# A's softmax chain at other steps of the block plan: three matches in the block in front, maxima and sums in four pieces, the exponential beside a product

## The chip, the cores and the metric

The kernel runs on one core of one Trainium2 chip. The metric is the device time of one execution in microseconds; of several runs the median is taken. Besides these runs there is one execution taken by the hardware profiler, from which all rows of the profile come. Its engines: PE multiplies matrices (PEld is its loading of weights), DVE is the vector engine, ACT the scalar engine, POOL is GpSimd, SP issues most of the DMA transfers. Each engine works through its own queue in order and waits there for semaphores of the others.

## The reference

Two attentions over inputs of 2048 x 576, with 32 heads of 18, side by side in the output:

```python
# A: each position attends to 8 positions, 2 apart, up to itself
qkv = (x @ wqkv)                       # q, k, v: heads x positions x 18
idx = pos[:, None] - arange(8) * 2     # masked where negative
logits = einsum("bhsd,bhswd->bhsw", q, k[idx]) * scale
o = einsum("bhsw,bhswd->bhsd", softmax(logits), v[idx]);  a = o @ wo
# B: full attention
p = softmax(einsum("bhqd,bhkd->bhqk", q, k) * scale)
o = einsum("bhqk,bhkd->bhqd", p, v);  b = o @ wo
out = concatenate([a, b], -1)
```

A and B have inputs and weights of their own.

## The kernel before

**Three stages.** First come the projections (x times wqkv for A and B), with part of B's maxima between the products. Then the main loop makes B's attention in 512 steps, and beside it, on engines' spare time, A's attention. At the end stand B's last output products.

**B's loop.** The 512 steps are 8 groups of four heads, times 4 blocks of 512 queries, times 16 tiles of 128 keys. A step (the `while step < ALL` loop at the end) makes four score products on PE (`score`, L263) and on ACT an exponential of each (L268); on PE the weighing with v of the step before (`weigh`, L731, all four heads into one PSUM tile `po`); and maxima for a later block: products of q and k on PE (`take`, L160), reduced on DVE (`reduce`, L168), worth three reductions of 128 x 512 a step. Scores, maxima and A's output products share seven PSUM banks in rings, so PE can only go on when ACT or DVE has given a bank back. When the 16 key tiles of a block are through (at steps 16, 32, 48 and so on), `finish` copies `po` out on ACT (L740), and plans the rest at fixed distances: the denominators go through DRAM (`den` loaded 1 step later, reciprocal on DVE 8 later, `drec` stored 9 later, `rec` loaded 13 later), and POOL multiplies and splits 18, 19 and 20 steps later (L767 to L769).

**The plan.** `plan(start, pieces)` and `later(n, f)` put functions on an agenda by step; `due()` runs those of a step at its end. What a function issues is thereby placed in the queues of its engines, behind all that earlier steps placed there. No engine waits for a step as such. POOL, with little of B's, may run ahead of the steps or behind them. SP too runs ahead until a transfer must wait, and what is queued behind that waits with it.

**A's blocks.** `local(j)` plans one of eight blocks of 256 positions, started at step 10 + 54 j. Its steps, counted from there, before the change:

- `fetch`: SP loads q (tile `aq`, one buffer) in four transfers from step -18 on, k (tile `akv`, two buffers, shared with v) from -10 on, and v from 16 on (for block 0: q from -9, k from -5).
- `match(c)`, c from 0 to 8: POOL multiplies q with the window of k (L868) and adds to the sum (L872), both 128 x 1024, at steps 5 to 25; the last makes the logits `lg` (L875, 128 x 512). The sum stays in the first of two `pr` buffers.
- `most`: DVE folds the eight window places into their maximum `am` in three pieces of 256, 128 and 64 elements a partition (L886) at steps 31, 32, 33.
- `lower`: POOL subtracts it (L892), step 33. `exponents`: ACT, one instruction of 128 x 512 (L895), step 35.
- `total`: DVE folds to the sum `as` the same way (L886), steps 36, 37, 38; `inverses`: two reciprocals on DVE (L902), 38 and 39. `share`: POOL multiplies (L905), 39.
- `weighted(c)`: POOL multiplies with v's window (L911) and adds three times (L912 to L914), steps 39 to 59; `upper` and `rest` split the result (L918, L923) at 60 and 61; `put` stores it at 64 and 66.
- `get`, `finished`: per block, four products with `wo` (two halves of columns for each 128 positions) are made at the steps that the table `MADE` names; `get` loads their input 8 steps ahead. `sums_of_a` puts a product into the next step's work, ahead of the fourth score: `beside` (L1036) makes its matrix products with two further maxima among them, ACT copies one sum (L954) and DVE adds the other (L955).

So a piece of A on DVE stands between two of B's reductions in DVE's queue, and one on ACT between two of B's exponentials.

Of the kernel before, what the change touches and what calls it, by code (L numbers as in the profile page):

```python
# [19 lines left out]
DH = 18  # L20
W = 8
# [21 lines left out]
GAP = 54  # L43

A_FROM = 10

MADE = ((88, 96, 112, 128), (144, 160, 176, 192), (201, 208, 224, 240), (250, 256, 272, 288),
        (304, 320, 336, 352), (361, 368, 384, 400), (412, 416, 432, 448), (466, 468, 475, 480))


def ap(t, *dims):

    return bass.AP(tensor=t.tensor, offset=t.offset, ap=[list(t.ap[0])] + [list(d) for d in dims])


def rows(t, *dims):

    return bass.AP(tensor=t.tensor, offset=t.offset, ap=[list(d) for d in dims])
# [3 lines left out]
def two_attentions(ctx: ExitStack, tc, xa, wa, woa, xb, wb, wob, out):  # L62
# [5 lines left out]
    nc = tc.nc  # L68
# [301 lines left out]
    with (tc.tile_pool(name="x", bufs=1, side="right") as xp,  # L370
# [103 lines left out]
        if True:  # L474
# [195 lines left out]
            for k in range(2, 14):  # L670
                n = 46 if k == 2 else 36 + 4 * k
# [7 lines left out]
            def leave_a(c, b, n, ps):  # L679
                o = xp.tile([128, 512], F32, name="ohi", bufs=4)  # L680
                nc.scalar.activation(o[:n], ps, AF.Copy)  # L681
                load(da[128 * c : 128 * c + n, HALO + 512 * b : HALO + 512 * b + 512], o[:n])
# [23 lines left out]
            for c, b in order:  # L706
                n = min(128, 3 * D - 128 * c)
                work_list.append(((b % 2, ws[c][0], xas[b][0], slice(0, n), every),
                                  lambda ps, n=n: ps[:n], lambda ps, c=c, b=b, n=n: leave_a(c, b, n, ps)))
# [109 lines left out]
    wo = {}  # L819

    producing = set()

    def load_wo(k, src, *pieces):

        raw = work.tile([128, D], F32, name="y", bufs=4)
        n = 0
        if len(pieces) == 4:
            nc.gpsimd.memset(raw, 0.0)
            n = 128
        for at, c0, m in pieces:  # L830
            load(raw[at : at + m], src[c0 : c0 + m])
            n = max(n, at + m)
        if k == "a":
            hi = work.tile([128, D], F32R, name="wohi", bufs=5)
            lo = work.tile([128, D], F32R, name="wolo", bufs=5)
        else:

            c = len(wo.get(k, []))
            hi, lo = (ap(t[:, 0, 0, :] if len(t.shape) == 4 else t[:, 0, :], (1, NB * 1024))[:, D * c : D * c + D]
                      for t in sets[(NG - 3) % 3])  # L840
        wo.setdefault(k, []).append((hi, lo))
        later(3, lambda: split_on(nc.gpsimd, hi[:n], lo[:n], raw[:n]))


    def local(j):

        st = {}
# [11 lines left out]
        def window(t, c):  # L859

            return ap(t[:, 2 * c, HALO:], (HALO + SUB, 2), (-DIL, W), (1, SUB))

        def wide():
            return work.tile([128, 2, W, SUB], F32, name="pr", bufs=2)

        def match(c):
            pr = wide()
            nc.gpsimd.tensor_mul(pr, ap(st["q"][:, 2 * c], (SUB, 2), (0, W), (1, SUB)), window(st["k"], c))  # L868
            if c == 0:
                st["pr"] = pr  # L870
            else:
                nc.gpsimd.tensor_add(st["pr"], st["pr"], pr)  # L872
            if c == DH // 2 - 1:
                lg = st["lg"] = work.tile([128, W, SUB], F32, name="lg", bufs=1)
                nc.gpsimd.tensor_add(lg, st["pr"][:, 0], st["pr"][:, 1])  # L875
                if j == 0:
                    for w in range(1, W):
                        nc.gpsimd.memset(lg[:32, w, : DIL * w], MASKED)

        def over_window(op, name, n):  # L880

            if n == 0:
                st[name] = work.tile([128, W // 2, SUB], F32, name=name, bufs=1)
            t, half = st[name], W >> n + 1
            src = t if n else st["lg"]
            nc.vector.tensor_tensor(t[:, :half], src[:, :half], src[:, half : 2 * half], op=op)  # L886

        def most(n):
            over_window(ALU.max, "am", n)
# [17 lines left out]
        def weighted(c):  # L907
            if c == 0:
                st["o"] = work.tile([128, DH, SUB], F32, name="ao", bufs=1)
            at = wide()  # L910
            nc.gpsimd.tensor_mul(at, ap(st["lg"], (0, 2), (SUB, W), (1, SUB)), window(st["v"], c))  # L911
            nc.gpsimd.tensor_add(at[:, :, :4], at[:, :, :4], at[:, :, 4:])  # L912
            nc.gpsimd.tensor_add(at[:, :, :2], at[:, :, :2], at[:, :, 2:4])  # L913
            nc.gpsimd.tensor_add(st["o"][:, 2 * c : 2 * c + 2], at[:, :, 0], at[:, :, 1])  # L914
# [10 lines left out]
        def put(i):  # L925
            load(rows(dao[j, i, 0, 0], (DH * SUB, 128), (1, DH * SUB)),
                 ap(st["parts"][i].bitcast(F32), (1, DH * SUB)))

        def get(n):
            st["x"] = []  # L930
            st["n"] = n
            last = work.tile([128, 128], F32R, name="ahl", bufs=1)
            for i in range(2):
                t = work.tile([128, 4, 128], F32R, name=f"at{i}", bufs=1)
                for s in range(2):
                    load(t.bitcast(F32)[:, :, SUB * s : SUB * s + SUB],
                         dao[j, i, 2 * n + s, :512].rearrange("(c p) n -> p c n", p=128))
                load(last.bitcast(F32)[64 * i : 64 * i + 64].rearrange("p (s n) -> p s n", s=2),
                     rows(dao[j, i, 2 * n, 512], (SUB, 64), (D * SUB, 2), (1, SUB)))
                st["x"].append([t[:, c] for c in range(4)])  # L940
            st["x"].append(last)
# [4 lines left out]
        def sums_of_a(h):  # L946
            his, los = zip(*wo["a"])
            w = his[:4], los[:4], his[4], los[4]
            cols = slice(288 * h, 288 * h + 288)
            if h == 0:  # L950
                st["y"] = ys["a", j, st["n"]] = work.tile([128, D], F32, name="y", bufs=4)
            one, two = beside("scores", *(halves(r, 0, w, st["x"], cols, slice(0, 128), True) for r in range(2)))
            y = st["y"][:, cols]
            nc.scalar.activation(y, two, AF.Copy)  # L954
            behind_scores.append(lambda: nc.vector.tensor_add(y, one, y))  # L955

        pieces = [(33, lower), (35, exponents), (39, share), (60, upper), (61, rest), (64, lambda: put(0)), (66, lambda: put(1))]

        pieces[:0] = [(at, lambda f=f, n=n: f(n)) for f, ats in ((most, (31, 32, 33)), (total, (36, 37, 38)),
                                                                (inverses, (38, 39))) for n, at in enumerate(ats)]  # L960
        for c in range(DH // 2):
            pieces.append((5 + 5 * c // 2, lambda c=c: match(c)))
            pieces.append((39 + 5 * c // 2, lambda c=c: weighted(c)))

        for nm, at, apart in (("q", -18, 2), ("k", -10, 2)) if j else (("q", -9, 1), ("k", -5, 1)):
            pieces += [(at + apart * i, lambda nm=nm, i=i: fetch(nm, i)) for i in range(4)]
        pieces += [(16 + 2 * i, lambda i=i: fetch("v", i)) for i in range(4)]
        made = [p - A_FROM - GAP * j for p in MADE[j]]
        for n, ends in enumerate((made[:2], made[2:])):
            pieces.append((max(ends[0] - 8, made[1] + 1 if n else 0), lambda n=n: get(n)))  # L970
            for h in range(2):
                pieces.append((ends[h], lambda h=h: finished(h)))
                producing.add(A_FROM + GAP * j + ends[h] + 1)
            pieces.append((ends[1] + 6, lambda n=n: load(out[p0 + 128 * n : p0 + 128 * n + 128, :D], ys["a", j, n])))
# [47 lines left out]
    def beside(kind, *both):  # L1022

        sums_ = [bank(k)[:, :288] for k in (kind, None)]
        turns = [[(sums_[r], *ab, i == 0, i == len(t) - 1) for i, ab in enumerate(t)] for r, t in enumerate(both)]
        pair = kind and sum(given) + 2 <= NG * NB * PIECES * 2
        if pair:

            for r in range(2):
                turns[r].insert(6 + 4 * r, None)  # L1030
        for i in range(max(map(len, turns))):
            for r in range(2):
                if i < len(turns[r]):
                    if turns[r][i]:
                        ps, a, b, start, stop = turns[r][i]
                        nc.tensor.matmul(ps, a, b, start=start, stop=stop)  # L1036
                    else:
                        maximum(r)()
        if pair:

            rings["else"].append(rings["else"].pop(0))
        return sums_
# [90 lines left out]
    rest = NG * NB * PIECES * 2 - early  # L1133

    total = early + rest
# [4 lines left out]
    while step < ALL:  # L1140
        n, kt = divmod(step, NT)
# [63 lines left out]
```

## Time and profile before

| | us |
|---|---|
| median of 3 runs | 1619.34 (1617.29 to 1619.95) |
| the profiled execution's own time | 1616.82 |
| its span | 1615.0 |
| PE, ACT, DVE, POOL busy | 1599.0, 1212.4, 1393.9, 961.1 |
| first exponential of the main loop's step 1 | 418.9 |
| first exponential of the last step | 1600.0 |

A row of the page's groups reads: line, engine, operation, tiles (written <- read), shapes and count, then busy us and mean ns of one, then the idle time of the engine just before them and what ended it. Instructions of an engine overlap a little, so busy time over count is less than the mean. In a view by stretches a row is: the stretch in us, its length, busy us and count of each engine that was asked for, the granted clock of PE (1.00 is full), the share of DMA and GB/s. A timeline row is: start, us, engine, line, operation, and in brackets the idle time before it with its releaser.

### The profile page before, as it was taken

Reading aid. Unit: us, or ns where it says so; the run is one execution under the profiler, and the core shown is the slowest. Engines: PE = TensorE matmul, PEld = TensorE weight load, DVE = VectorE, ACT = ScalarE, POOL = GpSimd, SP = SyncE. Lnnn points to the kernel's source line nnn. Section 1 sums busy time; section 2 is a strip of 40 time slices with the busy share of each in tenths; the row PEclk is TensorE's granted clock in tenths of the full one; section 3 lists DMA queues with packets and bytes.
Section 4 is the critical chain, followed back from the end, with each engine's and each line's share of the span. In section 5 each row is a group of like instructions: output and inputs, shape, how many; then the busy total and the mean of one; then the engine's idle time right before and its main releaser. Section 6 shows DMA issues by size and latency. Waiting matters only on the chain.

```text
span 1615.0 us, 35230 instructions
## 1 busy us (share of the span) xinstructions
PE 1599.0 (99%) x13394; PEld 959.5 (59%) x13394; DVE 1393.9 (86%) x2366; ACT 1212.4 (75%) x2419; POOL 961.1 (60%) x792
## 2 busy tenths in 40 slices
PE   9999999999999999999999999999999999999998
PEld 7999888999544444444444444444444444445676
DVE  5199999999899998999999999999999999999532
ACT  6424442121799998999999999999999999998444
POOL 2405742210265995996995995995996997920000
PEclk9999999999999999999999999999999999999999
DMA  8937954432222262254235235332532241034201
GB/s 250 239 121 196 275 164 133 134 104 79 60 56 64 73 147 54 62 118 113 62 85 133 72 98 115 98 91 60 125 106 58 59 135 47 22 124 139 89 38 60
DMA packets 186058, 172.11 MB, mean 107 GB/s; under 512 B 119152, under 2 KB 132976, under 8 KB 184160
## 3 DMA queue, kind: packets, MB, share of 16 engines
q1 hardware_dynamic: 181024, 158.31, 35.3%
q0 software_dynamic: 4032, 10.63, 3.1%
q8 instruction: 105, 1.72, 0.5%
q10 hardware_dynamic: 832, 0.92, 0.2%
q14 instruction: 65, 0.53, 0.1%
HBM read 96.94 MB, written 71.90 MB: 105 GB/s over the span
## 4 chain that ended last, share of the span: by engine, by line
PE 82%; POOL 7%; DVE 5%; DMA 3%; ACT 2%; issue 1%; SPq 0%; POOLq 0%; DVEq 0%; ACTq 0%
PE po L731 24%; PE bank L160 15%; PE bank L353 15%; PE bank L263 15%; PE bank L1036 8%; PE bank L290 5%; DVE mx L168 4%; ACT e L268 2%; POOL pr L868 1%; POOL pr L872 1%; POOL pr L911 1%; DMA akv<-da 1%; DMA dqk<-olo 1%; POOL pr L912 1%; POOL pr L913 0%
## 5 line engine op out<-in xcount | busy, mean ns | idle before, releaser
L168 DVE TENSOR_REDUCE mx<-bank 128x2 f32<-128x512 f32 x2048 | 1286.0, 684 | 114.5 <-PE bank L160 86.2
L268 ACT ACTIVATE e<-bank 128x512 f32<-128x512 f32 x2048 | 1050.2, 607 | 90.3 <-PE bank L263 83.2
L160 PE MATMUL bank<-ks,qs 54*128 54x256 f32 (+1 forms) x2536 | 791.8, 377 | 7.4 <-DVE mx L168 5.9
L160 PEld LDWEIGHTS bank<-ks,qs 54*128 54x128 f32 x2536 | 411.3, 184 | 464.6 <-DVE mx L168 423.4
L263 PE MATMUL bank<-qs,ks 56*128 56x512 f32 x2048 | 567.3, 426 | 0.1
L731 PE MATMUL po<-e,v 128*19 128x512 f32 x4096 | 537.9, 599 | 0.0
L263 PEld LDWEIGHTS bank<-qs,ks 56*128 56x128 f32 x2048 | 299.3, 185 | 14.7 <-issue 7.5
L868 POOL TENSOR_TENSOR pr<-aq,akv 128x1024 f32<-128x1024 f32 x72 | 158.5, 2202 | 15.4 <-DMA akv<-da 12.8
L911 POOL TENSOR_TENSOR pr<-lg,akv 128x1024 f32<-128x1024 f32 x72 | 158.5, 2201 | 0.6
L872 POOL TENSOR_TENSOR pr<-pr 128x1024 f32<-128x1024 f32 x64 | 152.6, 2384 | 5.0
L731 PEld LDWEIGHTS po<-e,v 128*19 128x19 f32 x4096 | 70.5, 97 | 129.4 <-issue 127.0
L681 ACT ACTIVATE ohi<-bank 128x512 f32<-128x512 f32 (+1 forms) x56 | 30.4, 595 | 152.5 <-issue 100.7
L353 PE MATMUL bank<-xhi,ahi 64*128 64x512 f32 (+1 forms) x448 | 113.5, 387 | 0.0
L353 PE MATMUL bank<-xhi,alo 64*128 64x512 f32 (+1 forms) x448 | 112.3, 387 | 0.0
L353 PE MATMUL bank<-xlo,ahi 64*128 64x512 f32 (+1 forms) x448 | 111.9, 388 | 0.1
L912 POOL TENSOR_TENSOR pr<-pr 128x512 f32<-128x512 f32 x72 | 92.5, 1285 | 5.6
L401 POOL TENSOR_TENSOR alo<-raw,ahi 128x512 fp32r<-128x512 f32 (+1 forms) x14 | 17.6, 1258 | 120.7 <-ACT ahi L400 88.8
L493 POOL TENSOR_TENSOR olo<-olo,ohi 128x512 fp32r<-128x512 f32 x36 | 46.2, 1294 | 66.1 <-ACT ohi L492 57.5
L767 POOL TENSOR_TENSOR o<-o,rec 128x512 f32<-128x512 f32 x29 | 37.6, 1297 | 58.7 <-ACT e L268 34.2
L103 POOL CAST mh<-mt 128x32 fp32r<-128x32 f32 x32 | 6.9, 217 | 102.3 <-DVE mt L183 99.5
L353 PEld LDWEIGHTS bank<-xhi,ahi 64*128 64x128 f32 (+1 forms) x448 | 65.0, 181 | 2.9
L353 PEld LDWEIGHTS bank<-xhi,alo 64*128 64x128 f32 (+1 forms) x448 | 63.9, 182 | 2.9
(197 smaller groups left out, 1827.6 us busy)
## 6 DMA issues: line engine op xcount, KB each, us to landing
do<-n SPq DMA_DIRECT2D x28, 512.0 KB
da<-ohi SPq DMA_DIRECT2D x52, 256.0 KB
akv<-da SPq DMA_DIRECT2D x64, 175.5 KB
out<-y SPq DMA_DIRECT2D x32, 288.0 KB
qs<-dqk SPq DMA_DIRECT2D x30, 288.0 KB
ks<-dqk SPq DMA_DIRECT2D x30, 288.0 KB
at<-dao SPq DMA_DIRECT2D x64, 128.0 KB
rec<-drec SPq DMA_DIRECT2D x29, 256.0 KB
```

Source lines behind the costliest of these rows:

```text
L160: return nc.tensor.matmul(ps if part is None else ps[:, 256 * r : 256 * r + 256], qs[at, b, p, 128 * t : 128 * t + 128], ks[at, p, 512 * k ...
L168: nc.vector.tensor_reduce(at, ps.rearrange("q (s n) -> q s n", s=2), axis=AX.X, op=ALU.max)
L263: nc.tensor.matmul(ps, ks[at, p, 128 * kt : 128 * kt + 128], qs[at, b, p], start=True, stop=True)
L268: nc.scalar.activation(e, ps, AF.Exp, scale=SCALE)
L290: nc.tensor.matmul(ps, a, b, start=c == i == 0, stop=c == 4 and i == 1)
L353: nc.tensor.matmul(ps, a, b, start=start, stop=stop)
L731: nc.tensor.matmul(po[32 * i : 32 * i + 19], vs[g][:, kt, 19 * i : 19 * i + 19], es[i], start=kt == 0, stop=kt == NT - 1)
L868: nc.gpsimd.tensor_mul(pr, ap(st["q"][:, 2 * c], (SUB, 2), (0, W), (1, SUB)), window(st["k"], c))
L872: nc.gpsimd.tensor_add(st["pr"], st["pr"], pr)
L911: nc.gpsimd.tensor_mul(at, ap(st["lg"], (0, 2), (SUB, W), (1, SUB)), window(st["v"], c))
L912: nc.gpsimd.tensor_add(at[:, :, :4], at[:, :, :4], at[:, :, 4:])
L1036: nc.tensor.matmul(ps, a, b, start=start, stop=stop)
```

## The change

In block j + 1, matches 0, 1 and 2 move from steps 5, 7 and 10 to -18, -17 and -15, that is to steps 36, 37 and 39 of block j (between `lower` and `share` there); matches 3 to 8 then stand at 11 to 23. Block 0 keeps its matches. The fetches of q and k move to -26 and -25 and on, one of each in turn. The maxima are folded in four pieces at steps 31 to 34 and the sums in four at 38 to 41: 128, 128, 128 and 64 elements in place of 256, 128 and 64. `lower` goes to 34, the exponential to 36, inverses to 42 and 43, share to 43, `weighted` to 43 to 63, `upper` and `rest` to 64 and 65, `put` to 68 and 70; in block 0 all these stand 4 steps earlier. Where `MADE` has a product at the exponential's step, the exponential is issued inside that product, in front of ACT's copy. `MADE` gets other steps for the first products of blocks 0, 3, 5 and 7, and `get` stands 6 steps ahead. Lines behind the new names shift by 3 to 13: `lower` is L897 in the changed kernel, `most` and `total` L890, `match` L871 and L875, `share` L910.

```diff
@@ -44,8 +44,8 @@
 
 A_FROM = 10
 
-MADE = ((88, 96, 112, 128), (144, 160, 176, 192), (201, 208, 224, 240), (250, 256, 272, 288),
-        (304, 320, 336, 352), (361, 368, 384, 400), (412, 416, 432, 448), (466, 468, 475, 480))
+MADE = ((96, 100, 112, 128), (144, 160, 176, 192), (201, 208, 224, 240), (256, 262, 272, 288),
+        (304, 320, 336, 352), (368, 370, 384, 400), (416, 424, 432, 448), (466, 468, 475, 480))
 
 
 def ap(t, *dims):
@@ -819,6 +819,9 @@
     wo = {}
 
     producing = set()
+    MADE_IN = {p for ends in MADE for p in ends}
+
+    beside_product = []
 
     def load_wo(k, src, *pieces):
 
@@ -881,9 +884,11 @@
 
             if n == 0:
                 st[name] = work.tile([128, W // 2, SUB], F32, name=name, bufs=1)
-            t, half = st[name], W >> n + 1
-            src = t if n else st["lg"]
-            nc.vector.tensor_tensor(t[:, :half], src[:, :half], src[:, half : 2 * half], op=op)
+
+            at, size, apart = ((0, 2, 4), (2, 2, 4), (0, 2, 2), (0, 1, 1))[n]
+            t, src = st[name], st[name] if n > 1 else st["lg"]
+            nc.vector.tensor_tensor(t[:, at : at + size], src[:, at : at + size],
+                                    src[:, at + apart : at + apart + size], op=op)
 
         def most(n):
             over_window(ALU.max, "am", n)
@@ -951,23 +956,31 @@
                 st["y"] = ys["a", j, st["n"]] = work.tile([128, D], F32, name="y", bufs=4)
             one, two = beside("scores", *(halves(r, 0, w, st["x"], cols, slice(0, 128), True) for r in range(2)))
             y = st["y"][:, cols]
+            while beside_product:
+                beside_product.pop()()
             nc.scalar.activation(y, two, AF.Copy)
             behind_scores.append(lambda: nc.vector.tensor_add(y, one, y))
 
-        pieces = [(33, lower), (35, exponents), (39, share), (60, upper), (61, rest), (64, lambda: put(0)), (66, lambda: put(1))]
-
-        pieces[:0] = [(at, lambda f=f, n=n: f(n)) for f, ats in ((most, (31, 32, 33)), (total, (36, 37, 38)),
-                                                                (inverses, (38, 39))) for n, at in enumerate(ats)]
-        for c in range(DH // 2):
-            pieces.append((5 + 5 * c // 2, lambda c=c: match(c)))
-            pieces.append((39 + 5 * c // 2, lambda c=c: weighted(c)))
-
-        for nm, at, apart in (("q", -18, 2), ("k", -10, 2)) if j else (("q", -9, 1), ("k", -5, 1)):
+
+        soon = 0 if j else 4
+        in_product = A_FROM + GAP * j + 36 - soon in MADE_IN
+        pieces = [(34, lower), (36, (lambda: beside_product.append(exponents)) if in_product else exponents),
+                  (43, share), (64, upper), (65, rest), (68, lambda: put(0)), (70, lambda: put(1))]
+
+        pieces[:0] = [(at, lambda f=f, n=n: f(n)) for f, ats in ((most, (31, 32, 33, 34)), (total, (38, 39, 40, 41)),
+                                                                (inverses, (42, 43))) for n, at in enumerate(ats)]
+        pieces += [(43 + 5 * c // 2, lambda c=c: weighted(c)) for c in range(DH // 2)]
+        pieces = [(at - soon, f) for at, f in pieces]
+
+        pieces += [(5 + 5 * c // 2 if not j else (-18, -17, -15)[c] if c < 3 else 11 + 5 * (c - 3) // 2, lambda c=c: match(c))
+                   for c in range(DH // 2)]
+
+        for nm, at, apart in (("q", -26, 2), ("k", -25, 2)) if j else (("q", -9, 1), ("k", -5, 1)):
             pieces += [(at + apart * i, lambda nm=nm, i=i: fetch(nm, i)) for i in range(4)]
         pieces += [(16 + 2 * i, lambda i=i: fetch("v", i)) for i in range(4)]
         made = [p - A_FROM - GAP * j for p in MADE[j]]
         for n, ends in enumerate((made[:2], made[2:])):
-            pieces.append((max(ends[0] - 8, made[1] + 1 if n else 0), lambda n=n: get(n)))
+            pieces.append((max(ends[0] - 6, made[1] + 1 if n else 0), lambda n=n: get(n)))
             for h in range(2):
                 pieces.append((ends[h], lambda h=h: finished(h)))
                 producing.add(A_FROM + GAP * j + ends[h] + 1)
```

## Prediction

> **What bounds the kernel now.** I read the head of the page first, then its costliest groups, and then cut the main loop into its steps by the exponentials of B (four `L268` to a step).
>
> ```profile
> span 1615.0 us, 35230 instructions
> ...
> PE 1599.0 (99%) x13394; PEld 959.5 (59%) x13394; DVE 1393.9 (86%) x2366; ACT 1212.4 (75%) x2419; POOL 961.1 (60%) x792
> ...
> L168 DVE TENSOR_REDUCE mx<-bank 128x2 f32<-128x512 f32 x2048 | 1286.0, 684 | 114.5 <-PE bank L160 86.2
> L268 ACT ACTIVATE e<-bank 128x512 f32<-128x512 f32 x2048 | 1050.2, 607 | 90.3 <-PE bank L263 83.2
> ...
> L868 POOL TENSOR_TENSOR pr<-aq,akv 128x1024 f32<-128x1024 f32 x72 | 158.5, 2202 | 15.4 <-DMA akv<-da 12.8
> ...
> L872 POOL TENSOR_TENSOR pr<-pr 128x1024 f32<-128x1024 f32 x64 | 152.6, 2384 | 5.0
> ```
>
> PE's 99% is not the answer: PE, DVE and ACT hand PSUM banks round in a ring, and each stands a little for the next. What a step costs, the busy time of the exponentials alone shows (stretch: us, busy and count, granted clock, DMA):
>
> ```profile
> 668.55:690.93 22.38, 22.38 (x45) 1.00 0.10 37
> 617.16:633.24 16.08, 8.46 (x17) 0.79 0.21 56
> 658.40:668.56 10.16, 8.30 (x17) 1.00 0.18 39
> 862.08:870.27 8.19, 8.11 (x16) 1.00 0.67 184
> 1343.01:1352.16 9.15, 8.23 (x17) 1.00 0.04 8
> 742.49:751.08 8.59, 8.13 (x17) 1.00 0.16 54
> 1100.90:1109.64 8.74, 8.17 (x17) 1.00 0.17 63
> ```
>
> The first row is eleven quiet steps: 22.38 / 11 = 2.035 us each. The others are four steps each, 8.14 when quiet; (the extra exponential in a count is one that the edge cuts). The reductions in the same eleven steps, by the same view cut to `L168`:
>
> ```profile
> 668.55:690.93 22.38, 20.77 (x34) 1.00 0.10 37
> ```
>
> They are 0.61 us each (20.77 / 34), three to a step and one cut by an edge: DVE is busy 1.83 to 1.89 of 2.035 us, so a step has only some 0.15 to 0.2 us of DVE to spare. Blocks of A put their maxima (`am`), sums (`as`) and inverses into that queue, in order with the reductions. The row 862.08 holds all three `am` of one block and costs 8.19 - 8.14 = 0.05: the ring absorbs about 0.9 us of DVE over such a stretch. What goes beyond is paid.
>
> **The dear place** is the second row: 16.08 us for steps 95 to 98, where the like four steps 111 to 114 (a block's start and a product in both) take 10.16. The timeline there, and two stretches of the plain windows:
>
> ```profile
> 621.31 1.26 POOL L875 TENSOR_TENSOR lg<-pr 128x512 f32<-128x512 f32 x1
> ...
> 622.61 0.43 DVE L886 TENSOR_TENSOR am<-lg 128x256 f32<-128x256 f32 x1 [3.38 <-POOL lg L875]
> ...
> 623.68 0.58 PE L160 MATMUL bank<-ks,qs 54*128 54x256 f32 x1 [2.85 <-DVE mx L168]
> ```
>
> ```profile
> 619.00:623.30 4.30, 1.83 (x16) 0.58 (x14) 0.92 (x3) 2.83 (x6) 3.49 (x2) 1.00 0.08 21
> 623.30:630.10 6.80, 6.42 (x41) 5.04 (x45) 4.95 (x9) 2.69 (x5) 0.00 (x0) 0.50 0.21 53
> ```
>
> POOL finishes the logits of A's block 1 too late, DVE stands 3.38 us before `am` with its reductions queued behind, PE stands 2.85, and then the granted clock is 0.50 for 6.8 us. So POOL, busy 60%, is what A's chain runs into.
>
> **What the change removes.** (1) The stall. POOL works without a pause from the share of block 0 to those logits:
>
> ```profile
> 522.06 1.28 POOL L905 TENSOR_TENSOR lg<-lg,as 128x512 f32<-128x512 f32 x1 [7.07 <-ACT e L268]
> ```
>
> The inverses of block 0 stay at steps 48 and 49, so its share stays there; but matches 0 and 1 of block 1 now stand ahead of it, in POOL's 7.07 us pause and the one ahead of `lower`. That is 2.20 + 2.20 + 2.38 = 6.8 us less behind it: the logits end at 622.6 - 6.8 = 615.8. `am` was asked for at 622.61 - 3.38 = 619.2; the product taken out of step 89 brings that to about 617.1 (its 2.07 follows below). POOL is 1.3 us early, and the stall goes: 10.16 - 16.08 = **-5.9**. Next late is what bounds any step, the ring.
>
> (2) The exponentials of a block (`L895`, one of 0.65 us on ACT). Stretches of `L268`, then of `L895`:
>
> ```profile
> 633.24:641.79 8.55, 8.12 (x17) 1.00 0.40 87
> 907.55:913.69 6.14, 4.32 (x9) 1.00 0.02 4
> 1226.98:1233.13 6.15, 4.31 (x9) 1.00 0.23 48
> ```
>
> ```profile
> 1226.98:1233.13 6.15, 0.63 (x1) 1.00 0.23 48
> ```
>
> Without a product (633.24, four steps) they cost 8.55 - 8.14 = 0.41. Beside one (1226.98, two steps of block 6, where it happened already) nothing: 6.15 against 6.14 for the same pair without them; and a product costs 6.14 - 4.07 = 2.07, the block's copy inside it. By step 36 of a block (32 in block 0) and the new table they fall beside a product in blocks 1, 3, 4, 6 and 7: four new ones, **-1.6**. The cover is ACT's idle time while PE makes the product; gone, it is 0.41 again.
>
> (3) `am` against POOL. Of two-input DVE operations that meet a running POOL operation the timeline shows:
>
> ```profile
> 1344.58 1.42 POOL L104 TENSOR_TENSOR ks<-y,qs 126x576 fp32r<-126x576 f32 x1
> ...
> 1344.97 1.31 DVE L886 TENSOR_TENSOR am<-lg 128x256 f32<-128x256 f32 x1
> ...
> 1345.96 1.46 POOL L767 TENSOR_TENSOR o<-o,rec 128x512 f32<-128x512 f32 x1
> ```
>
> `am` takes 1.31 and ends 0.28 after POOL's operation does, where the median of its eight is 0.42 (quoted below): it waits POOL out. Three blocks pay for such a meeting: 9.15, 8.59 and 8.74 above against 8.19, together 1.9. Which POOL operations lie there depends on when B's reciprocals land; POOL being earlier avoids some, not all. I take half, **-1.0**, between 0 and 1.9.
>
> **What it adds.** The `am` and `as` now are four pieces, not three:
>
> ```profile
> L886 DVE TENSOR_TENSOR am<-lg x8: 412/416/1306, 504.3 to 1345.0; 128x256 f32<-128x256 f32 x8
> ```
>
> ```profile
> L886 DVE TENSOR_TENSOR as<-as 128x128 f32<-128x128 f32 x8 | 2.2, 279 | 0.0
> ```
>
> The 0.42 becomes two of 0.28: +0.14 twice in eight blocks, 2.2 us of DVE, over one step more each with 0.15 to spare. I count 0; uncovered, 2.2. The products number as many at a block's start as before (96, 256, 368, 416 stay, the single ones move): 0. Fetches of q and k go 8 and 15 steps earlier in SP's queue, past `den` and reciprocal transfers; the buffer of q is free when match 8 has run, some 3 steps ahead of `lower`; one landing in the chain of waits is
>
> ```profile
> 477.81 5.32 DMA akv<-da
> ```
>
> 5.3 us, so eight issues and a landing end about when `lower` does: 0, with 1 to 3 us of POOL's time if late, which its pauses hold.
>
> **The new meeting.** POOL's pauses were what kept the sums clear of it:
>
> ```profile
> POOL lg L905 <- DVE as L902: 53.3, 6, 11.7
> POOL lg L892 <- DVE am L886: 38.8, 6, 10.5
> ```
>
> Between `lower` and the share POOL was idle 7 to 12 us while DVE made the sums and inverses. Now it goes from `lower` straight into matches 0 to 2 of the next block: 3 x 2.20 + 2 x 2.38 = 11.4 us, in some blocks with B's 3.2 us among them. In block 2 of before
>
> ```profile
> 749.64 1.27 POOL L892 TENSOR_TENSOR lg<-lg,am 128x512 f32<-128x512 f32 x1
> ...
> 755.09 0.42 DVE L886 TENSOR_TENSOR as<-lg 128x256 f32<-128x256 f32 x1
> ```
>
> the first sum comes 4.2 us after `lower` ends, three steps of the plan; now it is four, so 6.2, or with the exponentials in a product 6.2 + 2.07 - 0.41 = 7.9. Both lie inside the 11.4. No row has a two-input DVE operation under a match; the nearest (above) is one under a 1.42 us operation. Bounds: nothing, if it slips between two, and all of 2.38. The first wait I take at its mean, half of 2.3 = 1.15, since 0.3 us of shift turns 0.1 into 2.2. Then DVE's piece and POOL's next operation start together: three reductions later (1.83) the next piece meets the rest of 2.20 or 2.38, about 0.4. Three pieces are caught in blocks 1, 2, 3, 5 and 6 (1.95 each), two in blocks 0 and 4 (1.55), none in 7, which has no next block: 5 x 1.95 + 2 x 1.55 = **+12.9**. Spare DVE time is already used by the pieces themselves, so I let it cost in full, as the row 1343.01 does (0.9 longer for 0.89 more in `am`). Ends: 7 x 0.6 = 4 and 7 x 2.9 = 20.
>
> [...]
>
> **Sum:** -5.9 - 1.6 - 1.0 + 12.9 = +4.4. The profiled execution took 1616.82 us (span 1615.0 and 1.8 around it) and would become 1621.2; the runs' median is 1619.34, 2.5 above it. As the forecast is of a median: 1619.34 + 4.4 = **1623.7 us**.
>
> **Rivals.**
> - *The ring absorbs the waits* (faster). If the 0.4 us waits vanish in the banks' slack, and half a microsecond of the first too, seven blocks pay 0.65 each: 4.5 - 8.5 = -4.0, **1615.3**. For it: the row 862.08, where 0.9 us of DVE costs 0.05. Against: 1343.01. It decides where a block's waits cost below 0.75 us (7 x 0.75 = 8.5 - 3.2). 18%.
> - *They cost about what the rest saves*: 1.2 us a block, 7 x 1.2 - 8.5 = 0, **1619.3**. 27%.
> - *POOL is late again at block 1.* The margin is 1.3 us; match 2 still stands behind the share, and a late landing of k there uses it up. Then -5.9 fails: **1629.6**. 8%.
> - *A wait stops the clock.* After 2.85 us of idle PE it was halved; after the 0.9 us near 1347 it was not (1.00 in 1343.01). A wait of 2.4 lies between. Two such cost 2 x (5.9 - 2.85) = 6: **1629.8**. 5%. [...]
> - The forecast: 42%.
>
> Telling 0.2% (3.2 us) from no change is about what a measurement of this kernel can do. Faster by more 18%, within 27%, slower 55%. Range: from the first rival, 1615, to past the two last, 1630; the far ends of the new waits (4 and 20) would give 1615 and 1631.
>
> **What would show it.** Steps 95 to 98 near 10.2 us and no stretch at clock 0.50: step 1 right. `L897`'s row followed by matches with no pause, and `as` pieces of over 1 us where 0.28 is normal, one to three in each of blocks 0 to 6: the new meeting. If `as` stays at 0.28, the matches do not run there and the first rival or better holds. If `as` is long but four-step stretches stay at 8.2, the ring absorbed it. Wrong altogether would be a long wait of POOL for `akv`, or SP queued behind the early fetches with B's reciprocal late.

## The result, and the profile after

| | before | after |
|---|---|---|
| median of five runs each, on one chip, us | 1617.29 (1615.92 to 1619.95) | **1635.91** (1633.88 to 1640.55) |
| ratio | | **1.0119**, 95% interval 1.0097 to 1.0140 |
| profiled execution, us; its span | 1616.82; 1615.0 | 1633.88; 1632.1 |

The changed kernel is 18.6 us slower. The forecast said slower, but by 4.4, and the time lies above its range.

The head of the page after, two of its groups, and below them four rows of the waits of POOL (what it waited for, us in total, times, longest):

```profile
span 1632.1 us, 35226 instructions
...
PE 1601.4 (98%) x13394; PEld 964.1 (59%) x13394; DVE 1402.9 (86%) x2382; ACT 1212.2 (74%) x2419; POOL 962.4 (59%) x792
...
L871 POOL TENSOR_TENSOR pr<-aq,akv 128x1024 f32<-128x1024 f32 x72 | 158.4, 2203 | 64.4 <-DMA akv<-da 58.8
```

```profile
POOL pr L871 <- DMA akv<-da: 58.8, 6, 22.4
...
POOL lg L897 <- DVE am L890: 42.2, 7, 9.5
...
POOL lg L910 <- DVE as L907: 20.9, 5, 7.2
POOL lg L910 <- DVE mt L183: 17.4, 1, 17.4
```

Busy times are those of before to within a per cent; the time is in waits. The waits of `share` (L905 before, L910 after) fell, as the prediction had it: 53.3 + 7.1 us before, 20.9 + 17.4 after, where the 17.4 is block 7's, which has no next block. Matches now fill that pause. But the matches themselves wait 58.8 us for k where they waited 12.8, once for 22.4.

**Where it comes.** Comparing the first exponential of each step in the two traces, after is 2.2 us ahead at step 112, 2.9 ahead at step 256, 10.9 behind at 272, 16.4 behind at 288, and 17.4 behind at the end. So two short stretches decide. The exponentials of B (`L268`) there, with steps 95 to 98 first, then 256 to 259, and 272 and 273 (columns as in the prediction):

```profile
617.40:627.66 10.26, 8.31 (x17) 1.00 0.83 133
976.41:999.02 22.61, 8.39 (x17) 0.77 0.16 51
1025.82:1037.51 11.69, 4.31 (x9) 0.85 0.75 169
```

The first took 16.08 in before: the stall that the change was predicted to remove is gone. The other two are new: 22.61 and 11.69, where such steps with a product take 10.2 and 6.14.

**The chain behind the first of them** begins 120 us earlier, with the transfers of block 4's q and k. SP's own timeline:

```profile
856.86 0.62 SPq L858 DMA_DIRECT2D aq<-da  x1
...
858.11 0.60 SPq L858 DMA_DIRECT2D akv<-da  x1
860.27 2.67 SPq L142 DMA_DIRECT2D ks<-dqk  x1
...
869.31 0.56 SPq L858 DMA_DIRECT2D akv<-da  x1
...
876.88 2.38 SPq L766 DMA_DIRECT2D rec<-drec  x1
...
880.17 2.69 SPq L858 DMA_DIRECT2D akv<-da  x1
882.96 3.43 SPq L763 DMA_DIRECT2D den<-o  x1
```

These eight fetches are planned at steps 200 to 207. At steps 193 to 204 the plan also has the twelve loads of B's group 5 (`stack_loads`, `L142` and `L143`, 288 KB each; the expectations below say sixteen), in the same queue. The last five of them stand between the fetches. So the eight issues reach from 856.86 to 882.86. Single issues last 1.9 to 2.7 us in place of 0.6 (two of the loads, `rec` and the last fetch), and in front of loads SP itself waits, by its view of waits from 856.8 to 882.9, for the landing of earlier loads:

```profile
SPq L142 <- DMA ks<-dqk: 4.2, 2, 2.4
SPq L142 <- DMA qs<-dqk: 3.4, 2, 1.9
```

The POOL timeline shows what waits for the last fetch:

```profile
868.63 1.28 POOL L897 TENSOR_TENSOR lg<-lg,am 128x512 f32<-128x512 f32 x1 [8.96 <-DVE am L890]
892.31 2.17 POOL L871 TENSOR_TENSOR pr<-aq,akv 128x1024 f32<-128x1024 f32 x1 [22.40 <-DMA akv<-da]
...
907.33 1.27 POOL L910 TENSOR_TENSOR lg<-lg,as 128x512 f32<-128x512 f32 x1
```

`lower` of block 3, then 22.40 us of nothing, then match 0 of block 4; and behind the three matches the `share` of block 3, which needs nothing of k. Its last input, an inverse on DVE, was there at 888.91 (the reciprocal at 888.57, 0.34 long); it ran at 907.33. POOL works in order, so block 3 is 18.4 us late from here on, `weighted` and all. At step 256 B's own copy on ACT, `o` (`L740`), meets a POOL that has not yet freed its buffer:

```profile
982.81 0.60 ACT L740 ACTIVATE o<-po 128x512 f32<-128x512 f32 x1 [4.31 <-POOL n L769]
```

```profile
976.00:983.00 7.00, 2.88 (x23) 1.29 (x23) 2.98 (x5) 2.69 (x6) 6.86 (x6) 0.89 0.00 0
983.00:990.00 7.00, 7.00 (x52) 5.09 (x56) 3.13 (x5) 3.35 (x8) 6.76 (x4) 0.62 0.30 112
```

(Plain windows: PE, PEld, DVE, ACT, POOL, clock.) PE works 2.88 of 7 us while POOL is busy 6.86: POOL is the bound here, as ACT's exponentials stand behind `o` in its queue. In the second row PE is busy all through, at a clock of 0.62. Directly behind come the logits of block 4, late in their turn. The waits view from 970 to 1040 has that wait and those of PE:

```profile
DVE am L890 <- POOL lg L878: 4.7, 1, 4.7
...
PE bank L160 <- ACTq L243: 4.1, 1, 4.1
PE bank L160 <- DVE mx L168: 4.0, 1, 4.0
PE bank L1049 <- DMA at<-dao: 3.5, 2, 2.9
```

At 272 the product waits 2.9 us for its input (`at<-dao`, `L1049`), and PE's clock drops once more, to 0.50 from 1033 to 1036.

### The profile page after: what moved, and what is told of

Same layout as the page of the kernel before. It is cut to its first block, busy times and chain, and to the rows that moved or that the text cites. A ratio compares the mean times of both kernels' runs of the same rounds, so it can differ in the third digit from the quotient of the medians.

```text
span 1632.1 us, 35226 instructions
## 1 busy us (share of the span) xinstructions
PE 1601.4 (98%) x13394; PEld 964.1 (59%) x13394; DVE 1402.9 (86%) x2382; ACT 1212.2 (74%) x2419; POOL 962.4 (59%) x792
## 4 chain that ended last, share of the span: by engine, by line
PE 81%; DVE 6%; DMA 5%; POOL 5%; ACT 2%; SPq 1%; issue 1%; POOLq 0%; DVEq 0%; ACTq 0%
PE po L731 24%; PE bank L160 15%; PE bank L353 15%; PE bank L263 15%; PE bank L1049 7%; PE bank L290 5%; DVE mx L168 4%; POOL pr L916 1%; ACT e L268 1%; DMA ks<-dqk 1%; DVE as L890 1%; POOL pr L917 1%; DMA do<-n 1%; DMA den<-o 1%; POOL xlo L401 1%
## 5 line engine op out<-in xcount | busy, mean ns | idle before, releaser
L268 ACT ACTIVATE e<-bank 128x512 f32<-128x512 f32 x2048 | 1050.1, 607 | 99.3 <-PE bank L263 91.4
L871 POOL TENSOR_TENSOR pr<-aq,akv 128x1024 f32<-128x1024 f32 x72 | 158.4, 2203 | 64.4 <-DMA akv<-da 58.8
L875 POOL TENSOR_TENSOR pr<-pr 128x1024 f32<-128x1024 f32 x64 | 152.4, 2382 | 5.0
L353 PE MATMUL bank<-xlo,ahi 64*128 64x512 f32 (+1 forms) x448 | 115.6, 388 | 0.1
L1049 PE MATMUL bank<-wohi,at 64*128 64x288 f32 x512 | 65.7, 307 | 3.5 <-DMA at<-dao 3.5
L353 PEld LDWEIGHTS bank<-xlo,ahi 64*128 64x128 f32 (+1 forms) x448 | 67.1, 182 | 2.9 <-POOL xlo L401 0.5
```

The costliest lines, as they stand in the source:

```text
L268: nc.scalar.activation(e, ps, AF.Exp, scale=SCALE)
```

## The experiments

Theory L: the early fetches of block 4 (and 5) stand among B's large loads in SP's queue, match 0 lands late, `share` stands behind it, and block 3 slips. Rivals: M, the new meeting of DVE's pieces with POOL's matches is dearer than forecast; G, the shortened lead of `get` and the moved products. All edits below are against the changed kernel, unless said otherwise.

**e1: B's loads later.**

```diff
-            plan(STEPS * (g - 2) + 1, [(n, f) for n, f in enumerate(stack_loads(g))])
+            plan(STEPS * (g - 2) + (17 if g in (5, 6) else 1), [(n, f) for n, f in enumerate(stack_loads(g))])
```

> Edit: the changed kernel, with the sixteen loads of q and k of B's groups 5 and 6 (288 KB each) planned 16 steps later, so that they no longer lie on the early fetches of A's blocks 4 and 5. Theory L (late landing: match 0 of block 4 stands 22.4 us for its k and block 3's share stands behind it): the waits of 22.4 and 15.2 us go, the stalls at steps 256 to 259 and 273 go, and of 1635.9 us about 19 are given back: 1617, between 1613 and 1622. Theory M (the forecast's: the time is lost in sums that meet a running POOL operation): nothing of that changes, 1636 +- 3. Theory G (the products wait because their loads stand 6 steps ahead and not 8): the product at 256 waits as before, 1636 +- 3.

Measured: **1619.65** (1617.82 to 1624.04), against 1617.30 for before on the same chip: ratio 1.0019 (1.0008 to 1.0031). Moving the twelve loads of each of two groups 16 steps back takes away 16.3 us. POOL at the same place, and the stretches of steps 256 to 259 and 272 to 273:

```profile
869.33 1.28 POOL L897 TENSOR_TENSOR lg<-lg,am 128x512 f32<-128x512 f32 x1 [9.05 <-DMA akv<-da]
871.99 2.20 POOL L871 TENSOR_TENSOR pr<-aq,akv 128x1024 f32<-128x1024 f32 x1 [1.38 <-DMA aq<-da]
...
891.57 1.28 POOL L910 TENSOR_TENSOR lg<-lg,as 128x512 f32<-128x512 f32 x1 [4.39 <-DVE as L907]
```

```profile
977.15:987.38 10.23, 8.37 (x17) 1.00 0.30 62
1016.03:1022.18 6.15, 4.31 (x9) 1.00 0.15 36
```

Match 0 runs 20.3 us earlier, `share` 15.8; both stretches are normal again, with the input of `get` at its shortened lead. L holds; M and G do not explain the size.

**e2: reductions with one input.** The maxima and sums are made by four reductions straight from `lg`, each over the eight window places of a quarter of the columns, at the same steps.

```diff
-            nc.vector.tensor_tensor(t[:, at : at + size], src[:, at : at + size],
-                                    src[:, at + apart : at + apart + size], op=op)
+            cols = slice(SUB // 4 * n, SUB // 4 * n + SUB // 4)
+            nc.vector.tensor_reduce(st[name][:, 0, cols], st["lg"][:, :, cols].rearrange("q w n -> q n w"),
+                                    axis=AX.X, op=op)
```

> Edit: the changed kernel, with each of the four pieces of maxima and sums made by one reduction over the eight window places (one SBUF input) for 16 positions, in place of a fold with two SBUF inputs. Same steps. Pieces should take about 0.29 us each (as the 128x16<-128x128 reduction of B does), also under a POOL operation. Theory L: the pieces' excess over their normal length in the profile after sums to some 8 us, which go; the stalls at 256 to 259 and 273 stay: 1628, between 1625 and 1631. Theory M at the forecast's price: 12.9 us go, 1623. If the ring of banks absorbs such waits: 1636.

Measured: **1630.22** (1625.27 to 1633.86), ratio 1.0080 (1.0053 to 1.0107). That is 5.7 us less than after. The four runs spread over 8.6 us, and the interval of the ratio overlaps that of after (1.0097 to 1.0140), so the size of the meetings is not settled by this run; e3 gives it.

**e3: both edits.**

> Edit: both edits, loads of groups 5 and 6 sixteen steps later and one-input reductions. Theory L with the meetings at 8 us: 1635.9 - 19 - 8 = 1609, between 1605 and 1614, below the kernel before (1617.3). Theory M: 1623. If the two overlap (a stall hides a meeting), a little above 1609.

Measured: **1610.00** (1607.59 to 1612.39), ratio 0.9954 (0.9936 to 0.9972). With the loads out of the way the meetings are worth 1619.65 - 1610.00 = 9.65 us, the smaller part beside the 16.3 of e1. The sums by their tile, in after and then in e3 (ns min/median/max, first and last start, forms):

```profile
L890 DVE TENSOR_TENSOR as<-lg x16: 276/322/1781, 511.1 to 1380.0; 128x128 f32<-128x128 f32 x16
L890 DVE TENSOR_TENSOR as<-as x16: 210/355/991, 516.8 to 1384.1; 128x128 f32<-128x128 f32 x8, 128x64 f32<-128x64 f32 x8
```

```profile
L889 DVE TENSOR_REDUCE as<-lg x32: 358/373/381, 511.8 to 1360.6; 128x16 f32<-128x128 f32 x32
```

In e3 the same matches run beside them (21 of the 32 pieces overlap an operation of a match), and each of 32 takes 0.36 to 0.38. The kernel pays 0.37 instead of 0.28 a piece, and gains by it: block 6's sums cost four steps 9.34 us in after and 8.31 in e3 (exponentials of B again, after and then e3):

```profile
1257.12:1266.46 9.34, 8.25 (x17) 1.00 0.00 0
```

```profile
1234.99:1243.30 8.31, 8.28 (x17) 1.00 0.00 0
```

**e4: block 4 without lead.** Block 4 alone gets its matches and fetches back at the old steps.

```diff
-        pieces += [(5 + 5 * c // 2 if not j else (-18, -17, -15)[c] if c < 3 else 11 + 5 * (c - 3) // 2, lambda c=c: match(c))
+        pieces += [(5 + 5 * c // 2 if j in (0, 4) else (-18, -17, -15)[c] if c < 3 else 11 + 5 * (c - 3) // 2, lambda c=c: match(c))
...
-        for nm, at, apart in (("q", -26, 2), ("k", -25, 2)) if j else (("q", -9, 1), ("k", -5, 1)):
+        for nm, at, apart in (("q", -18, 2), ("k", -10, 2)) if j == 4 else (("q", -26, 2), ("k", -25, 2)) if j else (("q", -9, 1), ("k", -5, 1)):
```

> Edit: the changed kernel, with block 4's matches and fetches of q and k alone at their old steps; all other blocks as changed. Theory L: block 3's share no longer stands behind a match that waits for a landing, so the 22.4 us wait and the stalls at 256 to 259 and 273 go; but block 4 gains no lead, and with its chain unchanged and block 3's share 4 steps later, its logits are some 6 us late once: 1617 to 1626. Theory M: block 3's sums met nothing in the profile after, so nothing to gain there: 1636 +- 3, and theory G says the same.

Measured: **1628.31** (1623.71 to 1630.13), ratio 1.0066 (1.0043 to 1.0089): above what L expected. Block 3 no longer slips, but without lead block 4's logits are late once: DVE waits 6.0 us for them, PE 6.6, and steps 258 and 259 take 9.0 and 3.6 us. I had put 6 us on that; e4 is 8.7 us above e1. Block 5's fetches also still stand among the loads of group 6 (its match 0 waits 8.8 us). Direction right, price wrong: one test of L that it passes only in part.

**e5: the fetches of blocks 4 and 5 in POOL's queue.** This tells two forms of L apart: SP's order, or the DMA engines' bandwidth, which this edit leaves as it was.

```diff
-            load(st[nm][32 * s : 32 * s + 32],
+            issue = nc.gpsimd.dma_start if j in (4, 5) and nm != "v" else load
+            issue(st[nm][32 * s : 32 * s + 32],
```

> Edit: the changed kernel, with the fetches of q and k of A's blocks 4 and 5 issued from POOL's own queue in place of SP's; the plan is the same. It parts theory L in two. L-order: the fetches are late because SP works in order and they stand there among B's loads (issued from 856.9 to 882.9 in the profile after); from POOL's queue, idle 9 us before block 3's lower, they are issued by about 866, the waits of 22.4 and 15.2 us shrink to a few us and the time falls to 1617 to 1624. L-bandwidth: the sixteen 288 KB loads fill the DMA engines, the fetches land as late whoever issues them, and the time stays at 1636 +- 4.

Measured: **1618.52** (1617.23 to 1625.02), against 1617.09: ratio 1.0015 (1.0003 to 1.0027). It is the order. POOL's timeline, and the landing in the DMA view (count, KB each, median us from issue to landing):

```profile
869.63 0.67 POOL L859 DMA_DIRECT2D akv<-da  x1
...
879.75 2.21 POOL L872 TENSOR_TENSOR pr<-aq,akv 128x1024 f32<-128x1024 f32 x1 [9.45 <-DMA akv<-da]
```

```profile
akv<-da POOLq DMA_DIRECT2D x8, 175.5 KB, 9.7
```

The last issue ends at 870.30 where it ended at 882.86 in after, 12.6 us earlier, and match 0 starts 12.6 us earlier; from that end to the match it is 9.45 us in both. So the landing is as slow as it was, and the whole gain is in the time of issue. The waits of blocks 4 and 5 shrink only to 9.4 and 9.2 us, not to the few that I expected; nearly all of the loss goes even so, with 1.7 us of DVE waiting for block 4's logits left.

**e6: the lead of `get` back** from 6 steps to 8 (`ends[0] - 8`).

> Edit: the changed kernel, with the products' loads (get) planned 8 steps ahead again in place of 6. Theory L: what delays the products is block 3 slipping ten steps, not two steps of a load, so 1636 +- 4. Theory G: the product at 272 finds its input, 3 to 9 us less: 1627 to 1633.

Measured: **1637.71** (1635.21 to 1638.54), ratio 1.0127 (1.0111 to 1.0142): no gain. Steps 256 to 259, 272 to 273, and 310 to 313 there:

```profile
978.02:1000.68 22.66, 8.39 (x17) 0.77 0.17 51
1027.50:1033.66 6.16, 4.32 (x9) 1.00 0.77 202
1111.49:1126.44 14.95, 8.19 (x16) 0.77 0.54 101
```

The wait at 272 does go, 11.69 to 6.16. But block 5, whose match 0 waits 16.1 us for `akv`, then makes its logits too late at 312: 14.95. In after step 312 takes 2.8 us, as the time had been lost at 272 already. The same lateness is paid at the next place. A wait that vanishes is no gain as long as the late one behind it stays late.

**e7: the matches back.** All matches and fetches of q and k at their old steps, the rest of the change kept.

```diff
-        pieces += [(5 + 5 * c // 2 if not j else (-18, -17, -15)[c] if c < 3 else 11 + 5 * (c - 3) // 2, lambda c=c: match(c))
-                   for c in range(DH // 2)]
+        pieces += [(5 + 5 * c // 2, lambda c=c: match(c)) for c in range(DH // 2)]
...
-        for nm, at, apart in (("q", -26, 2), ("k", -25, 2)) if j else (("q", -9, 1), ("k", -5, 1)):
+        for nm, at, apart in (("q", -18, 2), ("k", -10, 2)) if j else (("q", -9, 1), ("k", -5, 1)):
```

> Edit: the changed kernel, with all matches and all fetches of q and k at their old steps; chain, pieces, exponentials and products stay as changed. No wait for landings and no sums under matches then, but POOL loses its lead: the share stands 4 steps (8 us) later, where POOL had 1 to 3 us to spare per block, so every block from 1 on has its logits some 6 us late, with PE idle beyond 2.9 us and the clock halved each time. Expected 6 to 9 us in each of seven blocks: 1655 to 1680. If the retimed chain were harmless by itself: 1615 to 1620.

Measured: **1671.77** (1671.10 to 1675.09), ratio 1.0344 (1.0328 to 1.0359). With `share` and `weighted` four steps later, POOL makes the logits too late in blocks 1 and 3 to 7:

```profile
DVE am L890 <- POOL lg L878: 35.8, 6, 9.2
```

The expectation had all seven; in block 2 the logits come in time, and PE waits 4.1 us for a product's input. So the lead for matches is what carries the later chain; the chain's new steps cannot be had without it.

**e8: the kernel before with both edits of e3** (its three pieces as reductions of 16, 16 and 32 columns).

> Edit: the kernel before, with the loads of B's groups 5 and 6 sixteen steps later and maxima and sums by one-input reductions (three pieces at the old steps). A control for the run of both edits on the changed kernel (1610.0): if those edits alone made it fast, this comes near 1610; if it is the change's lead for POOL, freed of its two costs, the stall at steps 95 to 98 stays here and only the 1.9 us of maxima that met POOL go: 1615, between 1613 and 1618.

Measured: **1618.67** (1617.94 to 1620.20), ratio 1.0010 (1.0001 to 1.0020). The two edits alone bring nothing; the stall at steps 95 to 98 is still there (DVE stands 3.6 us before `am`, PE 3.0). What e3 gains is the change's own: the lead for POOL, freed of its two costs.

**e9: e5 and one-input reductions; e10: e3 again.** Is it better to move the fetches or the loads?

> Edit: the changed kernel, with the fetches of q and k of blocks 4 and 5 from POOL's queue and with one-input reductions; the loads of groups 5 and 6 at their old steps. If the landing and the meetings are the two costs and add, the meetings' 8 to 9.6 us go from 1618.5: 1609 to 1611, as with the loads moved (1610.0). Where POOL's issues (eight of some 0.8 us in two blocks) cost it its lead: 1612 to 1616.

> The same kernel as the run of both edits (loads of groups 5 and 6 sixteen steps later, one-input reductions), once more on this chip beside the former: 1610 +- 2 if it holds.

Measured, against 1617.41: e9 **1613.36** (1610.86 to 1617.24), 0.9980 (0.9971 to 0.9990); e10 **1609.13** (1608.20 to 1610.08), 0.9953 (0.9936 to 0.9969). With one-input reductions, issuing on POOL costs some 4 us of what moving the loads gives; with folds it cost none (e5 1618.52, e1 1619.65). The traces show about 2 of the 4: in e9 DVE still waits 2.2 us for block 4's logits, in e3 not at all. The rest is not settled. e3 is the best version, twice 0.5% below before.

## Why the prediction missed

**The step that failed** is the one on the fetches: "so eight issues and a landing end about when `lower` does: 0, with 1 to 3 us of POOL's time if late, which its pauses hold." Measured cost: 1635.91 - 1619.65 = 16.3 us. It failed at three points.
- I took one landing of 5.3 us and normal issues, and named only `den` and reciprocal transfers as what the fetches pass. I did not ask what else the plan puts into SP's queue at the new steps of each block. For five of the seven blocks no such loads are planned there, and match 0 waited at most 4.6 us for k. For block 4 it is twelve 288 KB loads, planned at steps 193 to 204: the issues took 26 us, and match 0 waited 22.40 us. Block 5 (fetches at steps 254 to 261, loads of group 6 from 257) waited another 15.2 us.
- "Which its pauses hold" is wrong where something urgent stands behind the waiting instruction. The pause was `share`'s own: it now lies behind match 0 on POOL, so lateness of block 4 became lateness of block 3.
- The price is then not the wait. POOL stood 22.4 us, far from PE. It was paid some 85 us later, at the next point where B needs POOL (`o` at step 256) and where DVE needs it (`am`), with a clock of 0.50 (983 to 986) and 0.58 (996 to 999) behind the two: steps 256 to 259 cost 22.61 - 10.23 = 12.4 more than in e1, steps 272 and 273 cost 5.5 more.

The prediction's last paragraph did name a long wait of POOL for `akv` as what would make it wrong altogether; no rival with a price was made of it. The prices above could have been bounded from the rows of before: the stall at 95 to 98 shows what late logits cost (5.9), and two or three of them are 12 to 18.

**The stall, -5.9: right.** 16.08 to 10.26, clock 1.00, in after, e1 and e3; its undoing (e7) makes such stalls in six of the seven blocks.

**The exponentials, -1.6: right by the rows.** In blocks 1, 4 and 7 after, the two steps with a product and the exponential in it cost what such a pair costs without it (6.14):

```profile
631.74:637.92 6.18, 4.20 (x9) 1.00 0.00 0
1005.12:1011.27 6.15, 4.18 (x9) 1.00 0.82 146
1371.97:1378.09 6.12, 4.18 (x9) 1.00 0.34 76
```

(`MADE` has new first products for blocks 0, 3, 5 and 6; the text ahead of the prediction has 7 in place of 6.)

**`am`, -1.0: not in after.** The pieces of all maxima were 2.2 us over their normal length in before, 2.3 in after (the longest is 1.12 us, in block 5) and 1.1 in e1. So the forecast's saving shows in DVE's time in e1 only, where blocks 4 and 5 are not late.

**The new meeting, +12.9: mechanism and length of the waits right, price too high.** The sums of block 0, DVE and then POOL:

```profile
511.12 0.28 DVE L890 TENSOR_TENSOR as<-lg 128x128 f32<-128x128 f32 x1
...
513.33 1.78 DVE L890 TENSOR_TENSOR as<-lg 128x128 f32<-128x128 f32 x1
...
516.83 0.47 DVE L890 TENSOR_TENSOR as<-as 128x128 f32<-128x128 f32 x1
...
519.02 0.66 DVE L890 TENSOR_TENSOR as<-as 128x64 f32<-128x64 f32 x1
```

```profile
512.76 4.39 POOL L871 TENSOR_TENSOR pr<-aq,akv 128x1024 f32<-128x1024 f32 x2 [3.04 <-DMA akv<-da]
517.23 2.37 POOL L875 TENSOR_TENSOR pr<-pr 128x1024 f32<-128x1024 f32 x1
```

One piece waits a match out, the next ones the rest of the operation that POOL started meanwhile: 1.5, then 0.2 and 0.4 (the prediction had 1.15 and 0.4). The three pieces end at 515.11, 517.30 and 519.68; the first match ends at about 514.9, the two operations behind it at 517.15 and 519.60. No row of before shows a wait under a match: the forecast's 1.15 and 0.4, and with them its 12.9, were the author's estimate. The 1.5 of the first piece is more than the 1.42 us operation of the prediction could make it wait. In after the excess of the sums' pieces over their normal length (0.28, and 0.21 for the last) adds to about 8 us, in blocks 0, 1, 2, 5 and 6; blocks 3 and 4 have none, since there the matches came too late to meet them. In e1 they come in time in all seven blocks (busy us and mean ns of the sums' pieces):

```profile
L890 DVE TENSOR_TENSOR as<-lg 128x128 f32<-128x128 f32 x16 | 15.1, 947 | 0.0
L890 DVE TENSOR_TENSOR as<-as 128x128 f32<-128x128 f32 x8 | 4.5, 557 | 0.0
L890 DVE TENSOR_TENSOR as<-as 128x64 f32<-128x64 f32 x8 | 3.1, 383 | 0.0
```

That is 22.7 us where eight blocks at normal length take 8.4: 14.3 us of waits, against 12.9 in the prediction. But e1 against e3 gives back 9.65 us only, net of what e3's longer pieces may cost. So the step "so I let it cost in full" is the one that was too high, as far as these two runs tell. The rest of the sum holds too: without the late landing, for which the forecast's sum of +4.4 stands, e1 measures 1619.65 - 1617.30 = +2.35; e3 against before, 1610.00 - 1617.30 = -7.3, stands for the rest of the change, where the sum had -8.5.

**The rivals.** None of the four came in as priced. Without the late landing, e1 lies between the second (0 against before) and the forecast (+4.4). "A wait stops the clock" had the right mechanism, at another place: the clock fell behind the waits of PE of 2.9 to 4.1 us at 256 to 272, not behind the meetings; the sums' stretches of blocks 0, 1 and 6 all show 1.00. Behind the shortest of these waits, 2.88 us, the clock was 0.50 (1033 to 1036), as it was behind the 2.85 us in before.

**Open:** whether the 16 steps of e1 are the best place for the loads, about half of what e9 loses against e3, and how much of the 14.3 us of waits the ring absorbs. These were not tried apart.

## What to carry to other kernels

Before moving a transfer, list everything that its queue holds at the new place, block by block, not for the typical block: one block that meets the large loads decides the sum. Where early work is put ahead of due work in an in-order queue, the due work inherits the early work's inputs; price it as if the input came late. A two-input DVE operation that falls under long POOL operations, as the sums do, was better written here as a reduction of one input, even at 0.09 us more for each: 9.65 us less in e3 than in e1. In the kernel before, where the sums met nothing, that brought nothing (e8).

## What the runs showed of the hardware

- An issue of a fetch on SP lasts 0.62 us in the median of 96 in after; the last of block 4's, among the 288 KB loads, took 2.7 us and `den<-o` behind it 3.4. One of block 3's fetches took 6.2 us at 734, behind the loads of group 4. What lengthens them was not tried. Match 0 could start 9.5 us behind the end of the last issue in after, 6.3 in e1.
- In block 0, DVE's piece that waited for a match did not wait for the next one too: the piece of 513.33 ends at 515.11, within the pair of matches that runs to 517.15. Three reductions (1.83 us) are nearly as long as a match (2.20), and the later meetings of that block stayed short: 0.2 to 0.5 us.
- A reduction of the window places, to 128 x 16 from 128 x 128, takes 0.37 us (0.36 to 0.38 for the 32 in e3); I had expected 0.29, which B's reduction of these sizes (L176) takes in before.
